# Block 1's later attention units in 32-query tiles with VectorE transposes

## The chip, the cores and the metric

One core of one Trainium2 chip runs the whole program. The metric is device time in microseconds, median of several runs; lower is better.

## The reference

Inputs q, k, v have shape (4 batches, 8 heads, 576 positions, 64). Heads 0 to 3 use a local causal mask (a query sees its own position and the 31 before it); heads 4 to 7 a strided one (a query sees earlier positions with the same remainder by 32, and itself). Cut to what matters:

```python
scores = np.matmul(q, k.transpose(0, 1, 3, 2)) / np.sqrt(64)
scores = np.where(masks[None], scores, -1e9)        # local for h < 4, strided for h >= 4
attn = softmax(scores)
x = np.matmul(attn, v).transpose(0, 2, 1, 3).reshape(2304, 512)
h = np.maximum(x @ w_in, 0.0)                       # (512, 2048)
x = (s * (h * h) + b) @ w_out                       # (2048, 512)
out = ((x @ w_a) * (x @ w_b)) @ w_out2              # (512, 1536) twice, (1536, 512)
```

## The kernel before

The weights come as 64-bit floats. For each 128x512 piece, ScalarE (L130, L111) and VectorE (L133, L136, L140, L112) turn the words into a float32 and split it into a high and a low half in TensorE's reduced float32 form; a product of such pairs takes three matmul passes.

The first MLP walks over five blocks of columns. Block 0 holds the first 128 positions of all four batches (512 columns); blocks 1 to 4 hold the other 448 positions of batches 0 to 3, cut to 384 or 512 columns (64 columns are carried to the next block). Each block runs 16 steps f = 0 to 15, one for each 128 columns of the hidden layer: `h_mm` (12 matmuls, tile `h`), ScalarE and VectorE for relu and square (tile `gt`), and `o_mm` of the step two before (12 matmuls, tile `acc`).

While block n-1 runs its 16 steps, the attention of block n is computed beside it, so block 1's attention lies beside block 0's steps. In block 0 alone the 32 pieces of w_in and w_out are converted too, two in each step, one or two steps before TensorE needs them. Block 0's step 0 starts at 31.54 us, block 1's at 134.13 us.

Each block has six attention units: four of the local heads (`near[0]` to `near[3]`: head pair 0 and 1 for the first 256 positions, then pair 0 and 1 for the last 192) and two of the strided heads (`far[0]`, `far[1]`). A unit is a generator, and `plan(n)` writes by hand at which step each of its stretches is issued: the numbers in `at_n` and `at_f` are added to a first step, 4i-1 for `near[i]`, 8i+1 for `far[i]`. The stretches of a step are placed behind `o_mm` of that step and ahead of `h_mm` of the next, and on TensorE they stand in that order.

Two forms of the units exist.

The older one (`local`, `strided`), used for block 1, has 64-query tiles. q and k are loaded with positions on partitions and transposed on TensorE against an identity (tile `pst`, then copies by ScalarE). In `local` for block 1 the mask is added on TensorE (a matmul of `lmask`), VectorE takes the maximum (L231), and ScalarE does four exponentials that also sum (L237). `strided` adds the mask on VectorE and does its softmax there (L243 to L254). The probabilities are transposed on TensorE (`ppt`) and multiplied with v (`po`).

The newer one (`local_pairs`, `strided_pairs`), used for blocks 2 to 4, has 32-query tiles, two laid side by side in the partitions. q and k are loaded in blocks of 32 columns, and one or two VectorE instructions transpose them:

```python
nc.vector.transpose(out=qkT[:, 0:nq + nk].rearrange("p (j c) -> p j c", c=STR), in_=qk)
```

The mask is added on VectorE (L419), then maximum, subtraction, one exponential on ScalarE, sum, reciprocal and product (L426 to L433). It has fewer `ppt` transposes, and twice as many matmuls of half the columns for scores (`pss`) and `po`.

Work on each engine is put into a fixed order when the program is built; `after(...)` and `in_order(...)` hold an instruction behind others in that order. SyncE's queue (SP) issues nearly all loads, those of the attention and those of the weights, in one order.

Of the kernel before, what the change touches and what calls it, by code (L numbers as in the profile page):

```python
# [25 lines left out]
def sparse_attention_two_mlps(  # L26
# [24 lines left out]
    TF = P  # L51
# [41 lines left out]
    def mm(*args, **kwargs):  # L93
        last_pe[:] = [nc.tensor.matmul(*args, **kwargs).ins]  # L94

    def mm_t(*args):
        last_pe[:] = [nc.tensor.transpose(*args).ins]  # L97
# [12 lines left out]
    def split(hi, lo, src):  # L110
        nc.scalar.activation(out=hi, in_=src, func=AF.Copy)  # L111
        return nc.vector.tensor_tensor(out=lo, in0=src, in1=hi.bitcast(F32), op=ALU.subtract)  # L112
# [45 lines left out]
    def x_tile(n):  # L158
        if n not in x_t:
            x_t[n] = xp[n % 2].tile([P, 2, KD, TR if n % 2 else TM], F32R, tag="x", name="x")  # L160
            if n and n % 2 == 0:
                nc.gpsimd.tensor_copy(out=x_t[n][:, :, :, 0:OVER], in_=x_t[n - 1][:, :, :, TR - OVER:])
        return x_t[n]

    def first_column(n):
        return OVER if n % 2 == 0 else 0

    QT = 64
# [89 lines left out]
    def window(src, bb, head, t0, nt):  # L258
        at = src[bb, head, t0:S, :]
        return bass.AP(at.tensor, at.offset, [[D, WK], [QT * D, nt], [1, D]])  # L260
# [10 lines left out]
    def local(bb, n, pair, t0, nt):  # L271

        nq, nk = nt * QT, nt * QT + STR
        mq, mk = (P, nk // 3) if nk % 3 == 0 else (nq // 2, nk // 2)
        cq, ck = nq // mq, nk // mk
        nu = -(-nt // 2)
        tl = lambda shape, name: lp.tile(shape, F32, tag=name, name=name)
        qk = tl([P, 5, 2, D], "qk")
        z = t0 + nq
        qn, kn = qk[:, 0:2], qk[:, 2:]  # L280
        for h in range(2):
            for dst, src, a, m in ((qn, q, t0, mq), (kn, k, t0 - STR, mk)):
                nc.sync.dma_start(
                    out=dst[:m, 0:(z - a) // m, h],
                    in_=src[bb, 2 * pair + h, a:z, :].rearrange("(c p) d -> p c d", p=m),
                )
        yield
        qkT = lp.tile([P, 9 * QT], F32, tag="lT", name="qkT")
        qT, kT = qkT[:, 0:nq], qkT[:, nq:nq + nk]
        for src, m, c, dst in ((qn, mq, cq, qT), (kn, mk, ck, kT)):  # L290
            ps = ps_a.tile([P, c, m], F32, tag="a", name="pst")
            for i in range(c):
                mm_t(ps[:, i], src[:m, i].rearrange("p h d -> p (h d)"), ident[:m, :m])
            nc.scalar.activation(out=dst.rearrange("p (c m) -> p c m", m=m), in_=ps, func=AF.Copy)
        yield
        vn = tl([WK, 4, 2, D], "vn")
        for h in range(2):
            nc.sync.dma_start(out=vn[:, 0:nt, h], in_=window(v, bb, 2 * pair + h, t0 - STR, nt))
        pss = [ps_a.tile([P, nu, WK], F32, tag="a", name="pss") for _ in range(2)]

        def put(alone):
            for j in range(2 * nu if alone else nt):
                i = min(j, nt - 1) * QT
                for h in range(2):
                    hr = slice(h * D, (h + 1) * D)
                    mm(
                        pss[h][j % 2 * QT:(j % 2 + 1) * QT, j // 2],
                        lhsT=qT[hr, i:i + QT], rhs=kT[hr, i:i + WK],
                        start=alone, stop=(alone or j >= nt - 2),
                    )  # L310

        pt = tl([P, 2, nu, WK], "lpt")
        yield from softmax(pt, pss, lmask, put, n == 1, pair == 0 and t0 == TF)
        yield
        ppt = ps_a.tile([WK, 2 * nu, P], F32, tag="a", name="ppt")
        for i in range(2 * nu):
            mm_t(ppt[:, i, :], pt[:, i // nu, i % nu], ident)
        pT = lp.tile([WK, 2, nu * P], F32, tag="lT", name="pT")
        nc.scalar.activation(out=pT.rearrange("p h t -> p (h t)"), in_=ppt.rearrange("p i t -> p (i t)"), func=AF.Copy)
        yield  # L320
        po = ps_a.tile([P, nq], F32, tag="a", name="po")
        for j in range(nt):
            for h in range(2):
                mm(
                    po[h * D:(h + 1) * D, j * QT:(j + 1) * QT],
                    lhsT=vn[:, j, h, :], rhs=pT[:, h, j * QT:(j + 1) * QT],
                    start=True, stop=True,
                )
        xt, c0 = x_tile(n), t0 - TF + first_column(n)
        split(xt[:, 0, pair, c0:c0 + nq], xt[:, 1, pair, c0:c0 + nq], po)  # L330
        yield
# [654 lines left out]
    steps = {}  # L986

    def plan(n):
        at_n = (-2, 0, 1, 1, 2, 3, 4) if n == 1 else (-3, 0, 1, 2, 3, 4)
        at_f = (-3, 0, 1, 2, 4, 5) if n == 1 else (-3, 0, 1, 2, 3, 5)  # L990
        near = [
            (
                4 * i - 1,
                local(0, n, i % 2, TF + i // 2 * 4 * QT, 4 - i // 2) if n == 1
                else local_pairs(n - 1, n, i % 2, TF + i // 2 * 8 * QS, 8 - i // 2 * 2),
                at_n,
            )
            for i in range(4)
        ]
        far = [(8 * i + 1, (strided if n == 1 else strided_pairs)(n - 1, n, i), at_f) for i in range(2)]  # L1000
        if n == 1:
            near[0] = (0, near[0][1], (-5, -3, 0, 1, 1, 2, 3))
            far[0] = (1, far[0][1], (-5, 1, 2, 3, 5, 7))
        if n == 2:
            near[0] = (-1, near[0][1], (-2, 0, 1, 2, 3, 4))
        for first_, gen, at in near + far:
            for t in at:
                steps.setdefault((n - 1) * NF1 + first_ + t, []).append(gen)
# [80 lines left out]
    for n in range(1, NB):  # L1089
        plan(n)  # L1090
# [91 lines left out]
    for pair in range(NP2):  # L1182
        acc = [ps_acc.tile([P, DM], F32, tag="acc", name="acc2") for _ in range(TB2 // P)]
        later_x, late = [], []
        for g in range(NG2):
            i = pair * NG2 + g
# [129 lines left out]
```

## Time and profile before

| | |
|---|---|
| device time, median of 3 runs | 900.44 us (900.24 to 900.62) |
| span of the profiled execution | 898.1 us |
| TensorE busy | 888.6 us (99%) |
| VectorE busy | 620.5 us (69%) |
| ScalarE busy | 401.4 us (45%) |
| mean granted TensorE clock | 1.000 |

The span goes from the first to the last instruction of the program; the 2.3 us between it and the median lie around it. The profiled execution has no device time of its own beside its span. Busy shares are means over stages with different limits: block 0's steps carry the conversions of the weights, the later ones don't.

### The profile page before, as it was taken

What the parts mean: (1) busy time and instruction counts of PE and PEld (TensorE: products, weight loads), DVE (VectorE), ACT (ScalarE), POOL (GpSimd) and SP (SyncE); (2) the same over time, 40 slices, a digit from 0 to 9 for tenths busy, and PEclk for the clock granted to TensorE, in tenths of its full rate; (3) what the DMA queues carried; (4) which work ended last, traced back from release to release, by engine and by line L of the source; (5) the groups of instructions that cost most, each with busy time, mean ns of one, the idle gap of its engine ahead of it and who ended that gap; (6) DMA issues with size and microseconds to landing.
All of it is one profiled execution on the core that took longest, in us unless ns stands there. A gap on an engine that the chain in (4) does not pass through costs nothing.

```text
span 898.1 us, 16348 instructions
## 1 busy us (share of the span) xinstructions
PE 888.6 (99%) x6166; PEld 793.8 (88%) x6166; DVE 620.5 (69%) x1263; ACT 401.4 (45%) x866; POOL 42.0 (5%) x120
## 2 busy tenths in 40 slices
PE   8999999999999999999999999999999999999997
PEld 6778889999888899998889999988999988999986
DVE  6898995676766777727665777765776765776741
ACT  6777774434333343353333445354334444333322
POOL 6000000000000010001100000000000000000000
PEclk9999999999999999999999999999999999999999
DMA  9965534656765666446666343423432221433010
GB/s 229 292 204 162 166 77 134 159 149 162 207 170 159 176 190 172 130 137 220 196 214 207 129 141 112 138 80 113 151 99 94 84 94 59 124 95 106 30 36 35
DMA packets 156606, 126.41 MB, mean 141 GB/s; under 512 B 102256, under 2 KB 131440, under 8 KB 156528
## 3 DMA queue, kind: packets, MB, share of 16 engines
q1 hardware_dynamic: 149840, 109.12, 43.3%
q0 software_dynamic: 4608, 15.73, 4.4%
q8 instruction: 48, 0.79, 0.4%
q10 hardware_dynamic: 2080, 0.52, 0.3%
q14 instruction: 30, 0.25, 0.1%
HBM read 100.17 MB, written 25.17 MB: 140 GB/s over the span
## 4 chain that ended last, share of the span: by engine, by line
PE 97%; ACT 2%; DVE 1%; issue 0%; POOL 0%; ACTq 0%; POOLq 0%
PE acc L94 38%; PE pp L94 29%; PE h L94 22%; PE po L94 2%; PE pss L94 1%; PE ppt L97 1%; PE fpo L94 1%; PE fps L97 0%; PE lull L94 0%; ACT raw L130 0%; ACT fpt L596 0%; PE fss L94 0%; PE pst L97 0%; PE fpp L97 0%; PE fpx L97 0%; ACT r L778 0%
## 5 line engine op out<-in xcount | busy, mean ns | idle before, releaser
L94 PE MATMUL pp<-x2w,wf 128*128 128x384 f32 x1512 | 265.8, 335 | 0.0
L94 PEld LDWEIGHTS pp<-x2w,wf 128*128 128x128 f32 x1512 | 263.0, 188 | 1.8 <-ACT u L596 0.4
L94 PE MATMUL h<-x,w 128*128 128x512 f32 (+1 forms) x960 | 217.0, 374 | 0.0
L94 PE MATMUL acc<-gt,w 128*128 128x512 f32 (+2 forms) x960 | 210.7, 368 | 1.0 <-ACT w L111 1.0
L94 PEld LDWEIGHTS acc<-gt,w 128*128 128x128 f32 x960 | 175.5, 188 | 24.1 <-ACT w L111 1.5
L94 PEld LDWEIGHTS h<-x,w 128*128 128x128 f32 x960 | 171.8, 188 | 24.2 <-DVE w L112 0.5
L94 PE MATMUL acc<-o2w,abt 128*128 128x512 f32 x648 | 150.5, 390 | 0.0
L94 PEld LDWEIGHTS acc<-o2w,abt 128*128 128x128 f32 x648 | 121.4, 188 | 24.6
L778 ACT ACTIVATE r<-h 128x512 f32<-128x512 f32 (+1 forms) x80 | 44.4, 554 | 153.2 <-PE h L94 144.4
L788 DVE TENSOR_TENSOR r<-r 128x384 f32<-128x384 f32 (+1 forms) x64 | 40.0, 625 | 91.2 <-ACT gt L785 91.1
L601 DVE TENSOR_TENSOR u<-pp,u 128x384 f32<-128x384 f32 x72 | 39.9, 555 | 64.8 <-PE pp L94 59.3
L596 ACT ACTIVATE u<-pp 128x384 f32<-128x384 f32 x36 | 17.7, 493 | 115.6 <-PE pp L94 115.6
L596 ACT ACTIVATE wf<-w2t 128x512 fp32r<-128x512 f32 x72 | 45.2, 628 | 21.2 <-PE pp L94 20.3
L601 DVE TENSOR_TENSOR wf<-w2t,wf 128x512 fp32r<-128x512 f32 x72 | 49.3, 685 | 0.3 <-ACT wf L596 0.3
L130 ACT ACTIVATE raw<-raw 128x512 f32<-128x512 f32 x66 | 42.7, 671 | 8.2 <-DMA raw<-in_moe_w_a_dram 6.6
L136 DVE SCALAR_TENSOR_TENSOR raw<-raw 128x512 uint32<-128x512 uint32 x66 | 44.4, 689 | 0.7
L789 DVE TENSOR_TENSOR gt<-r,gt 128x384 fp32r<-128x384 f32 (+1 forms) x64 | 40.0, 624 | 3.6
L601 DVE TENSOR_TENSOR wf<-w2r,wf 128x512 fp32r<-128x512 f32 x72 | 39.6, 549 | 0.0
L596 ACT ACTIVATE wf<-w2r 128x512 fp32r<-128x512 f32 x72 | 37.2, 517 | 4.5 <-PE pp L94 4.0
L601 DVE TENSOR_TENSOR abt<-dly,abt 128x384 fp32r<-128x384 f32 x36 | 19.8, 556 | 25.0 <-ACT abt L596 24.9
L596 ACT ACTIVATE abt<-c 128x384 fp32r<-128x384 f32 x36 | 18.9, 524 | 40.4 <-DVE c L601 40.4
L785 ACT ACTIVATE gt<-r 128x384 fp32r<-128x384 f32 (+1 forms) x64 | 36.5, 571 | 0.4
(149 smaller groups left out, 805.1 us busy)
## 6 DMA issues: line engine op xcount, KB each, us to landing
w2t<-w2s SPq DMA_DIRECT2D x36, 512.0 KB
w2r<-w2d SPq DMA_DIRECT2D x60, 256.0 KB
raw<-in_moe_w_out_dram SPq DMA_DIRECT2D x28, 512.0 KB
w2d<-w2s POOLq DMA_DIRECT2D x36, 256.0 KB, 4.3
raw<-in_moe_w_in_dram SPq DMA_DIRECT2D x16, 512.0 KB
raw<-in_moe_w_a_dram SPq DMA_DIRECT2D x12, 512.0 KB
raw<-in_moe_w_b_dram SPq DMA_DIRECT2D x12, 512.0 KB
w2s<-w2t POOLq DMA_DIRECT2D x12, 512.0 KB, 4.0
```

The source lines that it names most:

```text
L94: last_pe[:] = [nc.tensor.matmul(*args, **kwargs).ins]
L97: last_pe[:] = [nc.tensor.transpose(*args).ins]
L130: nc.scalar.activation(out=high.bitcast(F32), in_=high.bitcast(F32), func=AF.Copy, scale=HIGH_SCALE)
L136: nc.vector.scalar_tensor_tensor(out=low, in0=high, scalar=3, in1=low, op0=ALU.logical_shift_left, op1=ALU.bitwise_or)
L596: i = nc.scalar.activation(**kwargs).ins
L601: i = getattr(nc.vector, method)(**kwargs).ins
L778: relu = nc.scalar.activation(out=r, in_=ph, func=AF.Relu)
L785: nc.scalar.activation(out=hi, in_=r, func=AF.Square)
L788: nc.vector.tensor_tensor(out=r, in0=r, in1=r, op=ALU.mult)
L789: last = nc.vector.tensor_tensor(out=lo, in0=r, in1=hi.bitcast(F32), op=ALU.subtract)
```

## The change

In `plan(1)`, `near[2]`, `near[3]` and `far[1]` take the newer form (with 6 tiles of 32 queries in place of 3 of 64 for the two local ones). `near[0]`, `near[1]` and `far[0]` keep the older one. With the form goes the list of steps: `near[2]` and `near[3]` load one step earlier, `far[1]` transposes its probabilities one step earlier (step 12, not 13). Blocks 2 to 4 are as they were.

```diff
     def plan(n):
-        at_n = (-2, 0, 1, 1, 2, 3, 4) if n == 1 else (-3, 0, 1, 2, 3, 4)
-        at_f = (-3, 0, 1, 2, 4, 5) if n == 1 else (-3, 0, 1, 2, 3, 5)
+        old = lambda i, late: n == 1 and i < late
         near = [
             (
                 4 * i - 1,
-                local(0, n, i % 2, TF + i // 2 * 4 * QT, 4 - i // 2) if n == 1
+                local(0, n, i % 2, TF + i // 2 * 4 * QT, 4 - i // 2) if old(i, 2)
                 else local_pairs(n - 1, n, i % 2, TF + i // 2 * 8 * QS, 8 - i // 2 * 2),
-                at_n,
+                (-2, 0, 1, 1, 2, 3, 4) if old(i, 2) else (-3, 0, 1, 2, 3, 4),
             )
             for i in range(4)
         ]
-        far = [(8 * i + 1, (strided if n == 1 else strided_pairs)(n - 1, n, i), at_f) for i in range(2)]
+        far = [
+            (
+                8 * i + 1, (strided if old(i, 1) else strided_pairs)(n - 1, n, i),
+                (-3, 0, 1, 2, 4, 5) if old(i, 1) else (-3, 0, 1, 2, 3, 5),
+            )
+            for i in range(2)
+        ]
```

## Rows read from the trace of the kernel before

**Rows 1.** The page's part 1: busy time and share of the span by engine.

```profile
PE 888.6 (99%) x6166; PEld 793.8 (88%) x6166; DVE 620.5 (69%) x1263; ACT 401.4 (45%) x866; POOL 42.0 (5%) x120
```

**Rows 2.** Timeline of the weight loads (PEld), block 0's steps: start, us, instructions.

```profile
62.12 2.60 PEld L94 LDWEIGHTS h<-x,w 128*128 128x128 f32 x12
...
67.48 2.68 PEld L94 LDWEIGHTS h<-x,w 128*128 128x128 f32 x12
...
74.36 2.62 PEld L94 LDWEIGHTS h<-x,w 128*128 128x128 f32 x12
...
80.66 0.37 PEld L97 LDWEIGHTS pst<-ident,qk 96*128 96x128 f32 x4
80.99 2.59 PEld L94 LDWEIGHTS h<-x,w 128*128 128x128 f32 x12
...
87.31 1.01 PEld L94 LDWEIGHTS po<-spT,sv 72*64 72x64 f32 x32
88.39 2.61 PEld L94 LDWEIGHTS h<-x,w 128*128 128x128 f32 x12
...
123.41 2.68 PEld L94 LDWEIGHTS acc<-gt,w 128*128 128x128 f32 x12
...
134.13 2.06 PEld L94 LDWEIGHTS h<-x,w 128*128 128x128 f32 x12
```

**Rows 3.** The same view in block 2's steps 8 to 15 (512 columns too).

```profile
262.38 2.60 PEld L94 LDWEIGHTS h<-x,w 128*128 128x128 f32 x12
...
268.44 2.60 PEld L94 LDWEIGHTS h<-x,w 128*128 128x128 f32 x12
...
273.79 2.68 PEld L94 LDWEIGHTS h<-x,w 128*128 128x128 f32 x12
...
304.48 1.02 PEld L94 LDWEIGHTS po<-spT,sv 36*64 36x64 f32 x64 [0.17 <-issue]
...
311.79 2.06 PEld L94 LDWEIGHTS h<-x,w 128*128 128x128 f32 x12
```

**Rows 4.** Groups of instructions by form, VectorE: count | busy us, mean ns.

```profile
L501 DVE STREAM_TRANSPOSE sqkT<-sqk 128x512 f32<-128x512 f32 x6 | 4.2, 706 | 0.0
L502 DVE STREAM_TRANSPOSE sqkT<-sqk 128x576 f32<-128x576 f32 x6 | 7.5, 1257 | 0.0
L445 DVE STREAM_TRANSPOSE qkT<-qk 128x416 f32<-128x416 f32 x6 | 3.6, 603 | 0.0
L419 DVE TENSOR_TENSOR lpt<-pss,lmask 128x128 f32<-128x128 f32 x24 | 5.8, 283 | 1.0 <-PE pss L94 1.0
L427 DVE TENSOR_TENSOR lpt<-lpt,mx 128x256 f32<-128x256 f32 x12 | 5.0, 419 | 0.1
L231 DVE TENSOR_REDUCE mx<-pss 128x2 f32<-128x192 f32 x8 | 2.6, 351 | 0.0
L254 DVE TENSOR_TENSOR lpt<-lpt,sm 128x384 f32<-128x384 f32 x4 | 2.2, 556 | 0.1
L427 DVE TENSOR_TENSOR sqk<-sqk,mx 128x288 f32<-128x288 f32 x6 | 2.7, 456 | 0.1
L245 DVE TENSOR_TENSOR spt<-spt,mx 128x576 f32<-128x576 f32 x2 | 1.5, 774 | 0.0
```

**Rows 5.** Busy time by stretch: length, then PE, PEld, DVE, ACT, POOL.

```profile
74.40:134.10 59.70, 59.70 (x417) 48.16 (x414) 54.08 (x110) 44.47 (x97) 0.00 (x0) 1.00 0.56 152
...
134.10:139.60 5.50, 5.50 (x61) 4.59 (x57) 1.73 (x4) 1.55 (x4) 0.00 (x0) 1.00 0.29 62
```

**Rows 6.** Waits between 74 and 134.1 us: total, times, longest.

```profile
DVE w L112 <- ACT w L111: 4.6, 4, 1.4
```

**Rows 7.** Timeline of VectorE in block 0's step 14.

```profile
123.58 0.69 DVE L112 TENSOR_TENSOR w<-raw,w 128x512 fp32r<-128x512 f32 x1
...
125.39 0.69 DVE L112 TENSOR_TENSOR w<-raw,w 128x512 fp32r<-128x512 f32 x1
```

**Rows 8.** Timeline of SyncE's DMA issues in block 0.

```profile
89.86 6.47 SPq L376 DMA_DIRECT2D sv<-in_v_dram  x8
96.38 0.47 SPq L118 DMA_DIRECT2D raw<-in_moe_w_in_dram  x1
```

## The prediction, made before the changed kernel ran

> **What bounds the kernel now.** The page's part 1 comes first: TensorE is busy for 99% of the span and VectorE for 69% [rows 1]. These are means, and the change touches one stage alone, so the next views are of that stage: the three changed units do all their TensorE work in block 0's steps 7 to 15, from 74.36 us (step 7's `h`) to 134.13 us (block 1's first `h`) [rows 2]. There the weight loads stand back to back; a step with no attention behind it, step 5, takes 67.48 - 62.12 = 5.36 us for its 24 matmuls [rows 2]. TensorE does not wait for anyone, and what attention adds between `o_mm` and the next `h_mm` lengthens the stage one for one. But the table by stretch shows a second engine near its limit: VectorE is busy for 54.08 of 59.70 us in this stretch, because it converts the weights there, and drops to 1.73 of 5.50 us right behind it [rows 5]. So the reader is to see two things: TensorE sets the pace, and VectorE has only 5.6 us of idle time in nine steps. Of that, 4.6 us are waits for ScalarE within the conversion of a weight (four waits) [rows 6], time that other VectorE work can fill if it is ready.
>
> **TensorE's part.** The nine steps take 134.13 - 74.36 = 59.77 us; less 9 x 5.36 = 48.24 this leaves 11.53 us for attention [rows 2]. Two things in it stay: `near[1]`'s product with v in step 7, and `far[0]`'s in step 8. The first: step 7 lasts 80.99 - 74.36 = 6.63 us, 1.27 over the plain step, of which 0.33 are `near[2]`'s four transposes (80.66 to 80.99), so 0.94 stays. The second is 88.39 - 87.31 = 1.08 [rows 2]. The three units to be changed thus take 11.53 - 0.94 - 1.08 = 9.5 us of TensorE.
>
> The same three units in the newer form, with the same sizes and the same list of steps, are in the trace already: block 2's steps 8 to 15, where the matmuls also have 512 columns. Those eight steps take 311.79 - 262.38 = 49.41 us, a plain step there (step 9) 273.79 - 268.44 = 5.35; 49.41 - 8 x 5.35 = 6.6 us [rows 3]. TensorE saves 9.5 - 6.6 = 2.9 us. How stretches fall together in a step matters (each switch of the form of matmul leaves a short gap of 0.2 to 0.4 us), so I bound the saving by 2.6 and 3.3 and take 2.9.
>
> On this point a rule speaks against the change. `far`'s product with v has half the columns and twice the matmuls in the newer form, yet 64 weight loads there take 1.02 us and 32 in the older form 1.01 us [rows 2, 3]: 16 ns each against 32. The Trainium skill (TensorEngine Tiling (Array Packing), section Instruction Overhead) says that each matmul costs about 60 cycles at least and that one should not take a tiling factor from a dimension that is already small; at 2.4 GHz I estimate 25 ns each from it, and with about 100 more matmul instructions (by the code 58 in place of 34 in each local unit, 132 in place of 82 in the strided one) TensorE would lose some 2.5 us where the rows say that it gains 2.9. By that rule the time would be about 903 us; the rows of the same tiles contradict it, since they run at less than 25 ns each.
>
> **VectorE's part.** It gains three kinds of work [rows 4]. Transposes: 2 x 0.603 + 0.706 + 1.257 = 3.17 us. The local softmax: two mask additions of 0.283 and four passes (maximum, subtraction, sum, product, of which the row of 0.419 stands for all four) make 2.24 us in each unit, where there were two maxima of 0.351 and one product of 0.556, 1.26 us: 2 x 0.98 = +1.97 us. The strided softmax: its four passes fall from 0.774 (one row for four) to 0.456, -1.27 us. Sum +3.9 us. Small items go the other way: two short scalings in each local unit go, and the strided mask additions have half the elements; I put them at -0.5, an estimate from the element counts of those rows. Successive VectorE instructions also overlap a little. I take +3.0, with bounds 2.4 and 3.9.
>
> So VectorE would need 54.08 + 3.0 = 57.1 us in a stretch that shrinks to 59.7 - 2.9 = 56.8 us. It cannot do quite all of it there. What saves it: behind 134.1 us it is idle for 3.8 of 5.5 us [rows 5], and the last conversions (the pieces of `w_out` for steps 14 and 15) are not needed before block 1's steps have begun. What can't slip: the pieces needed by steps 11 to 13. The tightest that the trace shows is the low half of `w_out`'s piece 12, written from 123.58 to 124.27 us [rows 7], while TensorE's group that reads it starts at 123.41 and loads weights until 126.09 [rows 2]. It didn't stop, so the low half was read late in the group; the margin is under 126.09 - 124.27 = 1.8 us. If the added work ahead of that point fills idle time only in part, TensorE waits there or at `far[1]`'s probabilities, which now have one step less (step 12). I charge 0.3 us for that in the likeliest case.
>
> **ScalarE and the queues** cost nothing that lasts. ScalarE loses work (the `pst` copies, and the four exponentials with their sums become one) and was busy for 44.47 of 59.70 us only [rows 5]; that shortens the waits of rows 6. The SP queue issues 12 more loads for `far[1]` and 12 more for the two local units. The worst place: the eight loads of `sv` took 6.47 us to issue, ahead of the last four weight pieces [rows 8]; sixteen take about 13, an estimate, so these pieces are issued some 6.5 us later, near 103 us. The first of them is finished as a weight by 126.1 [rows 7], so there are still about ten microseconds for landing and conversion. If that cover were gone VectorE would wait for a load, at most those 6.5 us. `near[2]` and `near[3]` load a step earlier than before, ahead of their VectorE transposes, which block that engine's order if a load is late.
>
> **The sum.** 898.1 - 2.9 + 0.3 = 895.5 us of span; with the 2.3 us between span and median, 897.8 us.
>
> **The rivals.**
>
> VectorE takes back part. For: 57.1 us wanted in 56.8, and a conversion whose margin is under 1.8 us. Against: 4.6 us of idle time that is only waiting, and ScalarE relieved. TensorE then waits 1 to 2.7 us: 898.5 to 900.2 us. Chance 0.27.
>
> VectorE becomes the bound of this stage: the slower side. None of the idle time is filled, and its 3.0 to 3.9 us land ahead of the conversions for steps 12 and 13, which then come late by that less the margin (1.0 to 1.8 us), while TensorE wants them 2.9 us earlier. The block ends 1.2 to 2.9 us later than before, 901.6 to 903.3 us; it decides from the point at which VectorE fills less than about 1 us of the waits. Chance 0.12.
>
> The small matmuls cost more than the rows of block 2 show, so that TensorE gains nothing or loses (the rule above): 900 to 903 us. Chance 0.03, since the same tiles have been seen.
>
> A late load: the transposes of `far[1]` stop VectorE for up to the 6.5 us of the longer queue. Its own idle time of 4.6 us takes most of that; 1 to 3 us would be left to TensorE, 898.8 to 900.8 us. Chance 0.06.
>
> **How the numbers follow.** My forecast, TensorE's saving kept within about 0.7 us (897.1 to 898.5), has 0.52; its own range is that one. 0.2% is 1.8 us, about what a measurement of this kernel can tell from no change: faster means below 898.6. The forecast lies there, and a third of the first rival does: 0.60. Slower, above 902.2: the greater part of the second rival and little of the third, 0.10. The rest, 0.30, is within. The range of 8 in 10 goes from 896.9 (TensorE's upper bound of 3.3 and no wait) to 901.0, which takes in the first rival and leaves out most of the second.
>
> **What would show it.** Right: no `pst` behind step 7 on TensorE; the steps 7 to 15 total some 8.6 us over nine plain steps, block 1's first `h` at about 131.5 us; VectorE at or above 98% of the stretch, its waits for ScalarE's `w` shorter; block 1's steps on unchanged. Wrong: a wait of TensorE for VectorE's `w`, `sqk` or `qkT` in steps 8 to 14, or for a load; or the later blocks placed differently by more than a few tenths.

## The result and the profile after

The changed kernel takes 905.33 us (904.58 to 905.82, 4 runs) against 900.34 us: ratio 1.0052, 95% interval 1.0040 to 1.0064. It is slower by 5 us where 2.6 us of gain were forecast, and outside the range. The profiled execution's span grew from 898.1 to 902.9 us.

The page's part 1 of the changed kernel, beside [rows 1], shows that no engine became much busier:

```profile
PE 888.2 (98%) x6264; PEld 793.1 (88%) x6264; DVE 623.1 (69%) x1272; ACT 397.5 (44%) x847; POOL 41.9 (5%) x120
```

TensorE works about as long as before in a longer span: it waits. The timeline of its weight loads in block 0 shows where (start, us, instructions):

```profile
74.61 2.62 PEld L94 LDWEIGHTS h<-x,w 128*128 128x128 f32 x12
...
96.18 2.68 PEld L94 LDWEIGHTS acc<-gt,w 128*128 128x128 f32 x12
103.23 0.20 PEld L97 LDWEIGHTS ppt<-ident,lpt 128*128 128x128 f32 x2 [4.38 <-issue]
...
104.37 3.88 PEld L94 LDWEIGHTS h<-x,w 128*128 128x128 f32 x12
108.29 2.69 PEld L94 LDWEIGHTS acc<-gt,w 128*128 128x128 f32 x12
...
111.91 2.60 PEld L94 LDWEIGHTS h<-x,w 128*128 128x128 f32 x12
...
126.43 2.68 PEld L94 LDWEIGHTS acc<-gt,w 128*128 128x128 f32 x12
130.20 0.20 PEld L97 LDWEIGHTS ppt<-ident,lpt 128*128 128x128 f32 x2 [1.09 <-issue]
...
138.11 1.01 PEld L94 LDWEIGHTS h<-x,w 128*128 128x128 f32 x6
```

Up to step 9 all goes as forecast. At step 10 the group of `acc` ends at 96.18 + 2.68 = 98.86 us, and the next load, the transposes of `near[2]`'s probabilities, comes at 103.23. At step 14 the same happens with `near[3]`'s, for 1.09 us. Behind the long wait the 12 loads of `h` take 3.88 us where they take 2.60 one step later. Block 1's first `h` comes at 138.11, not at 134.13 [rows 2] or the 131.5 that I named.

The waits between 74 and 140 us name what TensorE waited for, L433, the last pass of the local softmax; the second row answers to [rows 6]:

```profile
PE ppt L97 <- DVE lpt L433: 4.7, 2, 4.0
...
DVE w L112 <- ACT w L111: 4.3, 4, 1.5
```

The table by stretch (length, PE, PEld, DVE, ACT, POOL, granted clock, DMA) shows VectorE's load, beside [rows 5], and the clock behind the wait:

```profile
74.60:138.10 63.50, 58.82 (x515) 47.01 (x513) 56.56 (x117) 40.77 (x79) 0.00 (x0) 0.97 0.53 142
...
103.50:106.00 2.50, 2.50 (x70) 2.03 (x69) 2.50 (x7) 0.83 (x2) 0.00 (x0) 0.55 1.00 336
106.00:109.00 3.00, 3.00 (x13) 2.37 (x12) 2.96 (x7) 1.67 (x4) 0.00 (x0) 0.81 0.99 397
```

VectorE is busy for 56.56 us, 2.5 more than before, but it is also idle for 6.9 of the 63.5 us: it has time in this stretch, though not where TensorE waits. And TensorE, idle for 4.4 us, got a granted clock of 0.55, close to the lower of its two levels (1.2 GHz), and then 0.81, until it was at the full one again.

The timeline of VectorE shows why L433 is late. These are all the passes of `near[2]`'s softmax and some of what stands between:

```profile
88.36 0.48 DVE L419 TENSOR_TENSOR lpt<-pss,lmask 128x128 f32<-128x128 f32 x2
...
89.09 0.60 DVE L445 STREAM_TRANSPOSE qkT<-qk 128x416 f32<-128x416 f32 x1
...
90.79 0.70 DVE L501 STREAM_TRANSPOSE sqkT<-sqk 128x512 f32<-128x512 f32 x1
91.42 0.38 DVE L426 TENSOR_REDUCE mx<-lpt 128x4 f32<-128x256 f32 x1
...
93.45 1.27 DVE L502 STREAM_TRANSPOSE sqkT<-sqk 128x576 f32<-128x576 f32 x1
94.56 0.41 DVE L427 TENSOR_TENSOR lpt<-lpt,mx 128x256 f32<-128x256 f32 x1
...
97.36 0.41 DVE L430 TENSOR_REDUCE sm<-lpt 128x4 f32<-128x256 f32 x1
...
99.49 0.16 DVE L431 TENSOR_SCALAR sm<-sm 128x4 f32<-128x4 f32 x1
99.56 1.28 DVE L140 SCALAR_TENSOR_TENSOR raw<-raw 128x512 uint32<-128x512 uint32 x2
100.76 0.17 DVE L432 RECIPROCAL sm<-sm 128x4 f32<-128x4 f32 x1
100.85 0.65 DVE L112 TENSOR_TENSOR gt<-r,gt 128x512 fp32r<-128x512 f32 x1
101.43 0.75 DVE L133 TENSOR_SCALAR raw<-raw 128x512 uint32<-128x512 uint32 x2
102.10 0.68 DVE L112 TENSOR_TENSOR w<-raw,w 128x512 fp32r<-128x512 f32 x1
102.70 0.41 DVE L433 TENSOR_TENSOR lpt<-lpt,sm 128x256 f32<-128x256 f32 x1
```

From the first mask addition to the product 14.8 us pass, of which the passes themselves take 2.4. Most of the other 12 us are conversions, `gt`, the split of input columns (`x`), and the transposes of `near[3]` and `far[1]`, which stand between the dependent passes in VectorE's order. VectorE never stops in this time; each short pass just waits for its turn. (ScalarE's exponential, 0.42 us from 95.01 on, lies between the subtraction and the sum; VectorE works on conversions meanwhile.) In the kernel before, `near[2]`'s older chain ran from 88.08 to 93.79 us in the same place: fewer passes behind each other, with the mask and the sums on other engines. Its first and last pass, from that kernel's VectorE timeline:

```profile
88.08 0.61 DVE L231 TENSOR_REDUCE mx<-pss 128x2 f32<-128x192 f32 x2
...
93.23 0.56 DVE L254 TENSOR_TENSOR lpt<-lpt,sm 128x384 f32<-128x384 f32 x1
```

### The profile page after: what moved, and what is told of

Read it like the earlier page. It is cut to its first block, busy times and chain, and to the rows that moved or that the text cites. A ratio compares the mean times of both kernels' runs of the same rounds, so it can differ in the third digit from the quotient of the medians.

```text
span 902.9 us, 16570 instructions
## 1 busy us (share of the span) xinstructions
PE 888.2 (98%) x6264; PEld 793.1 (88%) x6264; DVE 623.1 (69%) x1272; ACT 397.5 (44%) x847; POOL 41.9 (5%) x120
## 4 chain that ended last, share of the span: by engine, by line
PE 83%; issue 7%; DVE 4%; ACT 3%; DMA 1%; POOL 1%; ACTq 0%; DVEq 0%; POOLq 0%
PE acc L94 32%; PE pp L94 29%; PE h L94 17%; PE po L94 1%; PE pss L94 1%; PE fpo L94 1%; PE ppt L97 1%; ACT raw L130 1%; DVE raw L136 1%; DMA w2d<-w2s 1%; DVE w L112 1%; POOL w2d L825 1%; DMA raw<-in_moe_w_a_dram 1%; ACT fpt L596 1%; DVE raw L140 1%
```

## The experiments

Theory A: the loss is the place of the local softmax in VectorE's order. A chain of dependent passes, the two mask additions and six behind them, has two steps until TensorE wants its result, and each pass stands behind a conversion. Theory B: VectorE has too much to do in these steps; wherever its work stands, TensorE waits for some of it.

**The local units alone** (`far[1]` in its older form):

```diff
-                8 * i + 1, (strided if old(i, 1) else strided_pairs)(n - 1, n, i),
-                (-3, 0, 1, 2, 4, 5) if old(i, 1) else (-3, 0, 1, 2, 3, 5),
+                8 * i + 1, (strided if old(i, 2) else strided_pairs)(n - 1, n, i),
+                (-3, 0, 1, 2, 4, 5) if old(i, 2) else (-3, 0, 1, 2, 3, 5),
```

> The change for the two local units alone; far[1] keeps the older form. Theory A (order): the softmax of near[2] is a chain of eight VectorE passes, each of which stands behind conversions of weights in VectorE's order, so that its probabilities come too late for step 10. The chain stays, only the 2.0 us of far[1]'s transposes leave its middle: a wait of about 2 us at step 10, 902 to 903.5 us. Theory B (amount): VectorE simply has too much to do in steps 7 to 10, and far[1]'s transposes are what overfills it: without them no wait over 0.5 us, 898.5 to 900.5 us.

Measured: 905.4 us, ratio 1.0053 (1.0040 to 1.0067). Neither came out in its numbers. `near[2]` was just in time at step 10, but `near[3]` was late at step 14, and the clock fell there in its turn. Timeline of the weight loads of this kernel:

```profile
127.79 0.20 PEld L97 LDWEIGHTS ppt<-ident,lpt 128*128 128x128 f32 x2 [3.19 <-issue]
...
129.74 3.74 PEld L94 LDWEIGHTS h<-x,w 128*128 128x128 f32 x12
```

So `far[1]`'s transposes decide at which step it happens, and the whole loss is there without them.

**`far[1]` alone** (both `old(i, 2)` of the local units made `old(i, 4)`):

> The change for far[1] alone; near[2] and near[3] keep the older form. Theory A: the older local softmax has five dependent VectorE passes and is in time; TensorE saves what far[1] saves, 1.5 to 2 us: 898.4 to 899 us. Theory B: VectorE gets 2 us of transposes in steps 8 and 9 and TensorE waits 1 to 2 us for a conversion or for probabilities: 900 to 901 us.

Measured: 900.26 us, ratio 1.0002 (0.9993 to 1.0010). The time is in B's range, but without the waits that B named. In block 0 it is as A says: no wait for a softmax in steps 7 to 15, and 1.3 us gained there (block 1's first `h` at 133.26 us against 134.13, with step 7 begun 0.45 us later). But the gain is lost behind it: block 1's first `h` waits for its last input columns, which VectorE and ScalarE split late, and a wait like it, of 0.7 us, returns at block 2's start.

```profile
135.65 0.30 PEld L94 LDWEIGHTS h<-x,w 128*128 128x128 f32 x2 [0.21 <-DVE x L112]
```

**One more step for `near[2]`:**

```diff
         if n == 1:
+            near[2] = (7, near[2][1], (-4, -1, 0, 1, 3, 4))
```

> All of the change, but near[2]'s scores one step earlier (step 7 in place of 8), so that its softmax has three steps in place of two before TensorE transposes it at step 10. No engine's work changes. Theory A: the 4.0 us wait at step 10 is gone and with it the low clock behind it (1.3 us); near[3]'s shorter wait at step 14 stays: 898.5 to 900 us. Theory B: the missing VectorE time shows as waits of 2 us or more elsewhere in steps 10 to 14: 901 to 904 us.

Measured: 899.80 us, ratio 0.9996 (0.9987 to 1.0005): 5.5 us below the changed kernel with the same work. The wait at step 10 is gone. TensorE waits for `near[3]` for 1.0 us at step 14 as A says; another 1 us, which A did not foresee, falls on `far[1]`'s transposes at step 12. Weight loads of this kernel:

```profile
98.52 0.37 PEld L97 LDWEIGHTS ppt<-ident,lpt 128*128 128x128 f32 x2
...
113.03 0.42 PEld L97 LDWEIGHTS ppt<-ident,sqk 128*128 128x128 f32 x4 [1.07 <-PE pss L94]
...
125.22 0.20 PEld L97 LDWEIGHTS ppt<-ident,lpt 128*128 128x128 f32 x2 [1.04 <-issue]
```

**The same work in another order**, conversions held behind the last pass that the local softmax has issued:

```diff
+        soon[:] = [last] if mark else soon          # behind the subtraction, and behind the product
...
-                with after(behind + (last_w if f == 1 else []) or last_act + last_dve):
+                with after(behind + soon + (last_w if f == 1 else []) or last_act + last_dve):
```

> All of the change, but the conversions of a step are held behind the last VectorE pass that the local softmax has issued so far (subtraction, then product) in VectorE's order. The same work, another order. Theory A: near[2]'s chain is about 4 us shorter, the wait at step 10 falls below 1 us: 898.5 to 900 us. Theory B: the conversions are late in its place, by as much: TensorE waits 3 us or more for a weight in steps 9 to 13: 902 to 905 us.

Measured: 899.51 us, ratio 0.9992 (0.9983 to 1.0001). `near[2]`'s product stands at 97.31 us, its first mask addition at 87.60: 10.1 us in place of 14.8. No wait for a weight appeared; at step 12 `far[1]`'s probabilities were late in place of it. Rows of this kernel's VectorE timeline and of its weight loads:

```profile
87.60 0.48 DVE L421 TENSOR_TENSOR lpt<-pss,lmask 128x128 f32<-128x128 f32 x2
...
97.31 0.42 DVE L436 TENSOR_TENSOR lpt<-lpt,sm 128x256 f32<-128x256 f32 x1
```

```profile
113.82 0.42 PEld L97 LDWEIGHTS ppt<-ident,sqk 128*128 128x128 f32 x4 [1.97 <-issue]
```

These two settle the main question: 5.5 to 5.8 us of the changed kernel's time come back with every instruction still there. They also give B its part: VectorE is so full (busy for 55.8 of the 58.9 us from step 7's `h` to block 1's first `h` in the run with one more step, 55.9 of 58.8 in this one) that, with one chain made early, other ones are late, by 2 us in all.

**Less VectorE work in the chain** (mask by TensorE, sums by ScalarE for block 1's two newer local units):

```diff
+                mm(pss[h], lhsT=ident_b, rhs=wide, start=True, stop=False)
...
+                nc.scalar.activation(
+                    out=pt[:, 0, x, 0:WS], in_=pss[h][:, b], func=AF.Exp, scale=scale,
+                    bias=mx[:, 2 * h + b:2 * h + b + 1], accum_out=sm[:, x:x + 1],
+                )
```

> All of the change, but block 1's two local units in the newer form get their mask by two matmuls on TensorE and their exponentials with sums on ScalarE, as the older form does. Their chain has five dependent VectorE passes in place of eight, and about 1 us less VectorE work each; TensorE gets 0.3 us more each. If the chains' length against the steps that they have is the cause: no wait for local probabilities at steps 10 and 14, a wait of 1 to 2 us for far[1]'s at step 12 may stay (it has a step less than before): block 1's first h at 132 to 133 us, 898.5 to 899.7 us. If VectorE's amount of work decides alone: 2 us less work takes 2 us off the 7 us of loss: about 903 us.

Measured: 899.25 us, ratio 0.9985 (0.9976 to 0.9994), block 1's first `h` at 132.45 us: as the length of the chains has it. No wait for local probabilities is left, one of 0.6 us stands at step 12. About two microseconds less VectorE work gave back 6. The Trainium skill (VectorE: DVE Perf Modes, section Rules for kernel authors) says of chained VectorE operations to keep their number small; these runs agree, for a reason of their own: each link costs a place in the order, here 1.1 to 2.8 us between one pass of `near[2]`'s softmax in the changed kernel and the next, and not only its own 0.2 to 0.5 us.

**`near[2]` earlier and `far[1]`'s probabilities a step later:**

```diff
+            near[2] = (7, near[2][1], (-4, -1, 0, 1, 3, 4))
...
-                (-3, 0, 1, 2, 4, 5) if old(i, 1) else (-3, 0, 1, 2, 3, 5),
+                (-3, 0, 1, 2, 4, 5) if n == 1 else (-3, 0, 1, 2, 3, 5),
```

> All of the change, with near[2]'s scores at step 7 (as in the run of that name) and far[1]'s probabilities transposed at step 13 as in the kernel before, not 12. TensorE loses 0.4 us of its saving by the extra gap. If the waits come from chains with too few steps: the wait at step 12 goes, near[3]'s at step 14 of 1 us stays: block 1's first h at 132 to 133 us, 898.5 to 899.5 us. If VectorE lacks time whatever the order: the 1 us wait of step 12 moves to step 13 or 14 and the time stays at 899.8 or above.

Measured: 902.38 us (900.27 to 904.00), ratio 1.0022 (1.0014 to 1.0031). This speaks for B: the wait at step 12 went, and `near[3]`'s at step 14 grew to 3.0 us. Its profiled execution, at 898.5 us of span, was among the quickest. That one and another, with a mean granted clock of 0.999, took 900.3 and 900.6 us; the other nine, with 0.996 to 0.998, took 901.9 to 904.0. So some 2 us of the median go with a lower clock that the profile does not show, and where it fell stays open.

```profile
126.28 0.20 PEld L97 LDWEIGHTS ppt<-ident,lpt 128*128 128x128 f32 x2 [2.97 <-issue]
```

**Fewer conversion passes:**

```diff
+        if short:                                   # w_out's pieces from 6 on
+            return high.bitcast(F32)
```

> All of the change, with work left out: from w_out's piece 6 on, VectorE's three passes that put the float32 together are left out (the piece stays as ScalarE scaled it), about 1.5 us less VectorE work in each of block 0's steps 7 to 15, so the output is not the reference's. If VectorE's chains are late because they stand among conversions: all waits of TensorE for VectorE in steps 7 to 15 vanish, block 1's first h comes at 131 to 131.5 us, 897 to 898 us (the full saving of TensorE). If something else holds the chains (ScalarE, the length of the chain itself, a load): the wait at step 10 stays over 2 us.

Measured: 897.75 us, ratio 0.9972 (0.9962 to 0.9982). Every wait of TensorE for VectorE in steps 7 to 15 is gone. Weight loads of this kernel:

```profile
131.19 2.06 PEld L94 LDWEIGHTS h<-x,w 128*128 128x128 f32 x12
```

Block 1's first `h` comes at 131.19 us, 2.94 before [rows 2]; 0.11 of that is an earlier start of step 7 (74.25 us against 74.36). The other 2.8 us are the saving of TensorE, with nothing taken back; and it is the presence of conversions between the passes that holds the chains, not the passes themselves. Since this kernel leaves work out, it does not tell order from amount; the runs with one more step and with another order do.

**Mask and sums elsewhere, `near[2]` earlier, `far[1]` a step later** (three of the edits above):

> The two local units with mask and sums as in the run of that name, near[2]'s scores at step 7 and far[1]'s probabilities at step 13. If the length of the chains against their steps is the cause, no wait over 0.5 us is left in steps 7 to 15: TensorE's saving is 2.9 less 0.4 (step 13) less 0.6 (mask): block 1's first h at 132.2 us, 898.3 to 898.8 us. If VectorE lacks time whatever is done, waits of 1 us or more stay: 899.3 us or above.

Measured: 898.79 us, ratio 0.9985 (0.9977 to 0.9994), block 1's first `h` at 132.47 us, the longest wait 0.5 us at step 14: as the first theory has it, at the upper end.

**The same without the later step for `far[1]`:**

> The two local units with mask and sums as in the runs of that name, near[2]'s scores at step 7, far[1]'s probabilities at step 12 as the change has it. If VectorE's chains are all in time now: no extra gap at step 13, block 1's first h at 131.6 to 132.2 us, 898.0 to 898.6 us. If far[1] with two steps is late whenever VectorE is this full: a wait of 0.5 to 1 us at step 12, no better than 898.8 us.

Measured: 899.66 us, ratio 0.9992 (0.9983 to 1.0001), with a wait of 1.3 us at step 12: `far[1]` with two steps is late while VectorE is this full.

**And with conversions held behind the local softmax:**

> As the run before, with the conversions of a step also held behind the local softmax in VectorE's order. If the order of VectorE is what is left: block 1's first h at 131.6 us, 898 us. If what is left are conversions that come late instead: 899 us or above, with waits of TensorE for a weight.

Measured: 898.22 us, ratio 0.9976 (0.9967 to 0.9985), no wait of TensorE for VectorE over 0.4 us in steps 7 to 15. Block 1's first `h` comes 0.6 us later than expected: step 7 begins 0.2 us later than before, and the mask's matmuls are on TensorE. This version beats both kernels.

```profile
113.00 0.42 PEld L97 LDWEIGHTS ppt<-ident,sqk 128*128 128x128 f32 x4
...
132.20 2.06 PEld L94 LDWEIGHTS h<-x,w 128*128 128x128 f32 x12
```

**TensorE kept at work through its wait** (the changed kernel otherwise):

```diff
+        if n == 1 and pair == 0:
+            spare = ps_a.tile([P, 3 * P], F32, tag="a", name="spare")
+            for _ in range(22):
+                mm(
+                    spare.rearrange("p (i c) -> p i c", i=3), lhsT=ident_b,
+                    rhs=ident_b[:, None, :].to_broadcast([P, 3, P]), start=True, stop=True,
+                )
         ppt = ps_a.tile([P, 2, P], F32, tag="a", name="ppt")
```

> All of the change, with 22 matmuls that nobody reads put ahead of near[2]'s transposes at step 10, so that TensorE works through its wait. VectorE's order stays nearly the same, the probabilities come no sooner. If 1.3 us of the loss are the lower granted clock behind the wait and not the wait: the granted clock stays 1.00 behind step 10, the next 12 loads of h take 2.6 us in place of 3.88, and the time is 1 to 1.5 us below the changed kernel's, 903.5 to 904.5 us. If the slow matmuls there have another cause (the loads that ran at that time): they stay at 3.9 us and the time at 905 or above.

Measured: 904.51 us (902.69 to 905.33), ratio 1.0041 (1.0028 to 1.0053); mean granted clock of the profiled execution 1.000. There the probabilities come no sooner, but the loads of `h` behind them take 2.59 us:

```profile
98.82 3.37 PEld L94 LDWEIGHTS <-ident_b 128*128 128x128 bf16 x22 [0.26 <-issue]
102.95 0.20 PEld L97 LDWEIGHTS ppt<-ident,lpt 128*128 128x128 f32 x2 [0.77 <-PE spare L94]
...
104.01 2.59 PEld L94 LDWEIGHTS h<-x,w 128*128 128x128 f32 x12
```

The table by stretch has the clock at 1.00 for these loads, while the DMA engines are as busy as they were in the changed kernel (1.05 here, about 1.00 there):

```profile
104.00:106.60 2.60, 2.60 (x21) 2.17 (x12) 2.60 (x8) 0.90 (x2) 0.00 (x0) 1.00 1.05 382
```

So the 3.88 us were the granted clock and not the loads from memory that ran then. In the medians the difference, 0.8 us, is within the spread of these runs, because the clock stayed up in two of the five executions only: 902.69 and 902.98 us at a mean granted clock of 1.000 and 0.999, 904.51 to 905.33 at 0.998. What lowered it in the other three is not in the profile.

## Why the prediction was wrong

**TensorE's saving of 2.9 us was right.** Block 2's steps gave it, and the run with fewer conversion passes shows 2.8 with all of it kept. The small matmuls cost nearly what the rows said: the 64 loads of `far[1]`'s product with v took 1.15 us in that run and 1.26 in the changed kernel (1.02 in [rows 3]), 18 and 20 ns each; the rival by the rule of the Trainium skill (TensorEngine Tiling (Array Packing), section Instruction Overhead) falls.

**VectorE's added work was about right.** I took 3.0 with a lower bound of 2.4; VectorE is busy 2.5 us longer [rows 5].

**The step that failed is "I charge 0.3 us for that in the likeliest case".** I weighed VectorE's busy time against the length of the stretch and then looked for late work among the conversions, and at `far[1]`'s probabilities because they lost a step. Of the local softmax I counted the passes' time, not their places. Its passes depend on each other and are spread among conversions, so 2.4 us of passes need 14.8 us, and two steps give TensorE's transposes less. The waits measured 4.4 us at step 10 and 1.1 us at step 14. And VectorE, which I expected at 98% of the stretch or above, was busy for 89% of it: what TensorE waited for was a place in VectorE's order and not its total. The conversions, where I saw the tightest margin, were never waited for in the changed kernel.

**A term was missing: the clock.** I put TensorE's wait at its own length. It costs another 3.88 - 2.60 = 1.3 us behind step 10. The waits lengthen their steps by a little less than they last: from the end of `acc` to the next `h` step 10 takes 5.5 us and step 14 2.75, where the run with fewer conversion passes takes 1.3 and 1.75. In block 0 the sum is then -2.8 + 4.2 + 1.0 + 1.3, and 0.2 us from before step 7, 3.9 us; block 1's first `h` is 138.11 - 134.13 = 3.98 us later.

**"Block 1's steps on unchanged" was wrong by 0.8 us.** 0.5 of it falls on block 2's first step, where `h` waits for its last input columns, which VectorE splits at its end (L112). Timeline of the changed kernel:

```profile
213.24 0.67 ACT L130 ACTIVATE raw<-raw 128x512 f32<-128x512 f32 x1 [2.85 <-DMA raw<-in_moe_w_a_dram]
...
214.35 0.56 DVE L788 TENSOR_TENSOR r<-r 128x384 f32<-128x384 f32 x1 [3.60 <-ACT gt L785]
...
218.35 1.26 DVE L502 STREAM_TRANSPOSE sqkT<-sqk 128x576 f32<-128x576 f32 x1
...
220.50 0.41 DVE L112 TENSOR_TENSOR x<-po,x 128x64 fp32r<-128x64 f32 x2
...
220.97 0.30 PEld L94 LDWEIGHTS h<-x,w 128*128 128x128 f32 x2 [0.68 <-DVE x L112]
```

The same stretch of the kernel before:

```profile
208.01 0.69 ACT L130 ACTIVATE raw<-raw 128x512 f32<-128x512 f32 x1 [1.64 <-DMA raw<-in_moe_w_a_dram]
...
213.71 1.26 DVE L502 STREAM_TRANSPOSE sqkT<-sqk 128x576 f32<-128x576 f32 x1
...
215.87 0.41 DVE L112 TENSOR_TENSOR x<-po,x 128x64 fp32r<-128x64 f32 x2
```

VectorE has the same order in both, with one of `far`'s transposes ahead of that split. What differs is the start: ScalarE waits 1.2 us longer for a piece of `w_a` to be loaded, VectorE waits for ScalarE's `gt` behind it, and the split begins 2.3 us behind the start of that `h` (218.16) where it was 1.7 (214.14). In the seven traces in which this `h` waits, for 0.4 to 0.7 us, ScalarE waits 2.6 to 3.0 us for that piece; in the six in which it doesn't, 0.5 to 1.8. Why the piece comes later is not shown.

**The rivals.** The first, by which VectorE takes back part, put TensorE's waits at 1 to 2.7 us; 5.5 were measured. The slower one had the engine and the sign but the wrong work (conversions) and a price of 901.6 to 903.3 us; it left out the clock and the later blocks. Its chance of 0.12 was too small: the prediction's own numbers, 57.1 us wanted in 56.8, said that VectorE had no room for an order that makes a chain wait. (Each order tried here with all of that work left something late, the best ones about 2 us; with two units' masks and sums elsewhere, `near[2]` a step earlier and the conversions held back, nothing was.) The late load did not happen in block 0: the sixteen loads of `sv` took 7.3 us to issue, not 13, and neither TensorE nor VectorE waited for a load in this stretch.

What stays open: which chain is late under a given list of steps. The run with `far[1]` a step later moved 3 us to `near[3]`, and I could not have said so from the list.

## What to carry to other kernels

When an engine off the critical path is nearly full, count the dependent passes that a result needs and what stands between them in that engine's order, not the sum of their durations: here 2.4 us of work took 14.8 us. A form of an operation that is faster in a stage with room (block 2) can be slower in a stage without it; move the passes to an engine with room, give the chain another step, or hold the long independent work behind it, and look again at which chain is late next. And look at the granted clock behind a wait of TensorE: the slower matmuls there can add to its price, here 1.3 us to 4.4.

## What the runs showed of the hardware

A wait of 4.4 us on TensorE was followed by 5.5 us at a granted clock of 0.55 and 0.81, and 12 loads with their matmuls took 3.88 us in place of 2.60; with matmuls that nobody reads in the wait they took 2.59 in the profiled execution. In the run with the local units alone, a 3.2 us wait had the same behind it (3.74 us); the 3.0 us wait of the run with both steps moved was followed by loads at the usual pace in its profiled execution. The Trainium skill (TensorE: Matmul & The Clock Gate, section Why this matters for your kernels) warns of idle gaps between bursts of matmuls because the throughput drops behind them; the changed kernel and the run with the local units alone agree.

The 32 x 32 transposes of VectorE were not slow in themselves: 0.60 us for 128x416, as in the later blocks [rows 4].
